# Attention and MLP under a scheduler: w_in's loads placed ahead of block 2, attention paced by another rule, and another planned DMA rate

## The chip, the cores and the metric

The kernel runs on one core of a Trainium2 chip. The metric is the device time of one execution in microseconds, the median of five runs. One execution was also taken by the hardware profiler; all times inside the kernel come from it. Of the core's engines, PE is the matrix engine TensorE (PEld its weight loads), DVE is VectorE, ACT is ScalarE, POOL is GpSimd, and SP is the queue engine that issues most DMAs.

## The reference

Inputs are q, k, v of shape (4, 8, 768, 64) in float32 (batch, heads, positions, head dimension), w_in (512, 2048) and w_out (2048, 512). Attention looks at chunks of 32 keys and keeps, for each query, the six chunks with the highest upper bound. Its result, with heads side by side, goes through an MLP with softplus.

```python
k_chunks = k.reshape(B, H, nc, chunk, D)                # chunk = 32, nc = 24
k_min, k_max = np.min(k_chunks, axis=3), np.max(k_chunks, axis=3)
ub = np.sum(np.maximum(q[:, :, :, None, :] * k_min[:, :, None, :, :],
                       q[:, :, :, None, :] * k_max[:, :, None, :, :]), axis=-1)
ub = np.where(causal, ub, -1000000000.0)
top_chunks = np.argsort(ub, axis=-1)[..., -top_k:]      # top_k = 6
scores = scale * np.matmul(q, k.transpose(0, 1, 3, 2))
scores = np.where(sel & (pos[:, None] >= pos[None, :]), scores, -1000000000.0)
attn = softmax(scores)                                  # written out in the reference
x = np.matmul(attn, v).transpose(0, 2, 1, 3).reshape(B * S, H * D)
h = x @ w_in
g = np.maximum(h, 0.0) + np.log1p(np.exp(-np.abs(h)))
return g @ w_out                                        # (3072, 512) float32
```

## The kernel before

The 3072 rows are cut into 12 blocks of 256 queries, three for each batch. For a block, attention works on four pairs of heads (`attend(n, p)`), after a preparation (`prep(n)`) that makes the bounds and the mask, and the MLP makes 16 tiles of 128 hidden features (`mlp_h`) and two tiles of 128 output rows (`mlp_y`). The attention of blocks 0, 1 and 2 is the ramp; the loop then emits the MLP of block n followed by loads, preparation and attention of block n + 3.

**What sets the order.** Nothing is issued where it is written. Every step is a `Task` in a `Graph` with an engine, a planned duration, the tasks it depends on, the buffers it takes and a priority, which is its due time. `Graph.schedule` plays the graph through at build time: whenever an engine is free, it gets the ready task of the lowest priority whose buffers are free. The order that comes out on each engine is the order in the program, and each engine then runs its queue strictly in that order, waiting on semaphores. Planned times never reach the chip; only the order does. A transfer has a planned `dma` time (1.17 for a load of 256 KB, 1.15 for a DMA transpose) and the queues share the DMA engines by packet weights. VectorE operations marked `port=True` and GpSimd's operations are never planned at the same time.

**Due times.** `when_att[n, p]` and `when_mlp[n, i]` come from a loop that deals out units of attention (of blocks 3 to 11) and of the MLP, starting at `MSTART`; it takes a unit of attention as long as the share of attention dealt out is at most `AHEAD` times the share of the MLP:

```python
        if ia < len(a_units) and (im >= len(m_units) or ta / asum <= ahead * tm / msum):
```

`prep(n)` is due 14 ahead of the first attention unit of its block (for the ramp, `RLEAD[n]` ahead), its loads `LEAD` = 18 ahead. `POST[n]` puts back what follows the attention of ramp block n.

**Loads of the ramp.** `ORDER` lists them: `k0` is k of block 0 and so on, `i01` the first half of w_in, `o0` a quarter of w_out. Loads of q, k and v go out from SP (some of block 0's from ACT), the weights from POOL, which converts them to bf16 on the way. A weight that follows a load of q, k or v in the list is put behind a "hold": a copy of one element on POOL (line 428) out of the tile named in `HOLD`, so that POOL issues the weight only when that tile has landed. The other way round, SP's next loads wait for a two-element DMA out of a weight (`hold_sp`, line 434). `LGATE` is such a gate, behind the third quarter of w_out: all loads of blocks 3 to 11 (line 465) depend on it.

**The chain of a block from block 3 on.** Loads (L465) in float32; casts to bf16 on POOL (L472 for q and k, L470 for v); DMA transposes of k (L520) and q (L568) on SP; on DVE the chunks' minima and maxima (L524), their spread into `bd` (L541), the positive and negative parts of q (L577) and copies (L580, L530); the bounds on PE (L597, L598, `ub`); on DVE the causal addition (L604), the eight highest (L613), the comparison with the sixth (L621, L624) that gives the mask in `mr`; a DMA transpose of the mask (L660) and two copies into the q operands (L663). Then `attend`: scores on PE (L700), exponentials on ACT (L709), the causal cut of the last tile by an affine select on POOL (L715), attention times v (L726), normalisation on DVE (L735, L747), and a DMA transpose into x (L763). In the ramp the transposes are PE matmuls (L501, L558, L645, L755).

**The MLP.** `mlp_h`: L783 on PE with w_in, exponential and logarithm on ACT (L789, L793). `mlp_y`: L809 on PE with w_out, a copy on DVE (L814), the store from SP (L819).

**Fillers.** Until the planned time `WARM` = 30, where PE has nothing ready, the scheduler puts a matmul on zeros (L363) into one PSUM bank that is kept spare for it. They stand in the program like any other instruction.

PSUM has eight banks; `PSUM_CAP` limits how many each use may hold (`s` scores, `h` and `y` of the MLP, `o` attention results and bounds, `t` transposes of the ramp).

Of the kernel before, what the change touches and what calls it, by code (L numbers as in the profile page):

```python
# [16 lines left out]
B, H, S, D = 4, 8, 768, 64  # L17
# [3 lines left out]
NP = H // 2  # L21
# [11 lines left out]
NRAMP = 3  # L33
OHP = -97.5
W2 = 18
# [3 lines left out]
TLAT = 1.4  # L39
RLEAD = (0, 0, -1)  # L40
POST = (9, 2, -2)
OPRIO = 15.0
LEAD = 18
BG = 40
DMA_START = 1.3
MSTART = 10.0
AHEAD = 1.16
ORDER = "k0 q0 k1 v0 q1 v1 k2 q2 v2 i01 i23 o0 o1 o2 o3".split()
HOLD = ("k", 2, 1)

# [4 lines left out]
WIDE = {"xf", "kq", "kt", "mt", "oall"}  # L55
PSUM_CAP = {"s": 4, "h": 3, "y": 2, "o": 2, "t": 3, "l": 4, "kq": 4, "kt": 2, "mt": 2, "oall": 2}

# [15 lines left out]
class Graph:  # L73
# [39 lines left out]
    def schedule(self):  # L113
# [8 lines left out]
        def post(at, what, x):  # L122
            nonlocal seq
            seq += 1
            heapq.heappush(events, (at, seq, what, x))
# [35 lines left out]
        def flow(to):  # L161
            nonlocal moved
            while moved < to:
                live = [q for q in queues.values() if q]
                if not live:
                    moved = to
                    return
                slow = {id(q): q[0][2] if len(live) == 1 else q[0][2] + 1 for q in live}
                total = sum(slow.values())
                rate = {id(q): q[0][2] / total for q in live}  # L170
                step = min(min(q[0][0] / rate[id(q)] for q in live), to - moved)
                moved += step
                for q in live:
                    q[0][0] -= step * rate[id(q)]
                    if q[0][0] <= 1e-9:
                        t = q.pop(0)[1]
                        post(moved + t.lat, "landed", t)

# [90 lines left out]
def build(nc, tiles):  # L269
# [16 lines left out]
    for n in range(NRAMP):  # L286
        for p in range(NP):
            when_att[n, p] = t0 + p * (att[n] + 2.5) / NP
        t0 += att[n] + 2.5
    a_units = [(n, p, att[blocks[n][1]] / NP) for n in range(NRAMP, NB) for p in range(NP)]  # L290
    m_units = [(n, i, 13.9 / 16) for n in range(NB) for i in range(16)]
    asum, msum = sum(u[2] for u in a_units), sum(u[2] for u in m_units)
    ahead = AHEAD
    ia = im = 0
    ta = tm = 0.0
    now = MSTART
    while ia < len(a_units) or im < len(m_units):
        if ia < len(a_units) and (im >= len(m_units) or ta / asum <= ahead * tm / msum):
            n, p, d = a_units[ia]
            when_att[n, p] = now  # L300
            ia, ta, now = ia + 1, ta + d, now + d
        else:
            n, i, d = m_units[im]
            when_mlp[n, i] = now
            im, tm, now = im + 1, tm + d, now + d
# [73 lines left out]
    def v_dst(n, t):  # L379
        b, blk = blocks[n]  # L380
        return T("v", b % 2)[:, blk * NT + t, :, 0:D]
# [26 lines left out]
    def landing(nm, n, hh):  # L408
        return [(XF[nm, n, t], u) for t in ([hh] if n == 0 else range(NT)) for u in range(2)]


    def weight(nm, c4, k4, pr, after):
# [13 lines left out]
    def hold_pool(key, pr):  # L426
        b_ = XF[key]
        return [add("POOL", 0.15, lambda: PO.tensor_copy(T("scratch")[0:1, 0:1], T(b_)[0:1, 0:1]), pr,
                    r=[(b_, 0), (b_, 1)], w=["scratch"], name="hold")]

# [5 lines left out]

    gate, key, wgate, prev = (), None, (), []
    for k_, what in enumerate(ORDER):
        pr = -100 + k_ * 5
        if what[0] in "kqv":  # L440
            if len(prev) > 1:
                gate = hold_sp(*prev[-2], pr - 0.5)
            ramp_loads(what[0], int(what[1]), pr, gate)
            key, wgate, prev = HOLD, (), []
        else:
            nm, c4 = {"i": "w_in", "o": "w_out"}[what[0]], int(what[1])
            k4 = len(what) - 1
            if key:
                wgate, key = hold_pool(key, pr), None
            weight(nm, c4, k4, pr if nm == "w_in" else OPRIO + 0.1 * c4, wgate)  # L450
            prev.append((nm, c4))
    LGATE = hold_sp(*prev[-2], pr)

    def loads(n):
        base = when_att[n, 0] - LEAD
        b, blk = blocks[n]
        for i, nm in enumerate("kqv"):
            b_ = None
            if nm != "v":
                b_ = KQ[nm, n] = Buf("kq")  # L460
            for t in range(NT):
                xf = Buf("xf", "l")

                def ld(nm=nm, t=t, xf=xf):
                    SP.dma_start(out=T(xf).rearrange("s (h d) -> s h d", h=H), in_=rows(nm, n, t))  # L465
                add("SP", 0.6, ld, base + i, at=base + 0.5 * i, w=[xf], dma=1.17, lat=0.6, name=f"ld{nm}{n}", after=LGATE)

                def cast(nm=nm, t=t, xf=xf, b_=b_):
                    if nm == "v":
                        PO.tensor_copy(v_dst(n, t), T(xf).rearrange("s (h d) -> s h d", h=H))  # L470
                    else:
                        PO.tensor_copy(T(b_)[:, :, t], T(xf).rearrange("s (p c) -> s p c", p=NP))  # L472
                w = [("v", b % 2, blk * NT + t)] if nm == "v" else [(b_, t)]
                add("POOL", 0.6, cast, base + i + 2, r=[xf], w=w, name=f"c{nm}{n}")

    QAB, X, done = {}, {}, {}


    def prep(n):
        b, blk = blocks[n]  # L480
        i = b % 2
        ramp = n < NRAMP
        pr = when_att[n, 0] - (RLEAD[n] if ramp else 14)
        ncc = (blk + 1) * NCB
# [30 lines left out]
        else:  # L515
# [3 lines left out]
            def tr(ks=ks, kt=kt):  # L519
                SP.dma_start_transpose(T(kt), T(ks).rearrange("s p t c -> s (p t c)"))  # L520
            add("SP", TD, tr, pr, at=pr - 4, r=[(ks, 0), (ks, 1)], w=[kt], dma=1.15, lat=TLAT, name=f"kTd{n}")
            for m in range(2):
# [41 lines left out]
        else:  # L564
            qs = KQ["q", n]

            def tr(qs=qs):
                SP.dma_start_transpose(T(qb).rearrange("d p (t s) -> d (p t) s", t=NT),  # L568
                                       T(qs).rearrange("s p t c -> s (p t c)"))
            add("SP", TD, tr, pr + 0.5, at=pr - 3, r=[(qs, 0), (qs, 1)],  # L570
                w=[(qb, hh, z) for hh in range(2) for z in range(3)], dma=1.15, lat=TLAT, name=f"qTd{n}")
        for hs in ([[0], [1]] if ramp else [[0, 1]]):
# [83 lines left out]
        else:  # L656
            mt = Buf("mt")

            def tr(mt=mt):
                SP.dma_start_transpose(T(mt).rearrange("d p (t s) -> d (p t) s", t=NT),  # L660
                                       T(mr).rearrange("s p t c -> s (p t c)"))
            add("SP", TD, tr, pr + 3, r=[(mr, z) for z in range(3)], w=[mt], dma=1.15, lat=TLAT, name=f"mTd{n}")
            add("DVE", 0.36, lambda: DV.tensor_copy(T(qa)[64:96], T(mt)[64:96]), pr + 3,  # L663
# [15 lines left out]
    def attend(n, p):  # L679
# [82 lines left out]
        elif p == NP - 1:  # L762
            add("SP", TD, lambda: SP.dma_start_transpose(  # L763
                T(x).rearrange("d p (t s) -> d (p t) s", t=NT), T(osb).rearrange("s p t h d -> s (p t h d)")), pr + 1.5,
                r=[(osb, p_) for p_ in range(NP)], w=[(x, p_) for p_ in range(NP)], dma=1.15, lat=TLAT, name=f"oTd{n}")

# [62 lines left out]
    for n in range(NB):  # L829
        m = n + NRAMP  # L830
        mlp_h(n)
        mlp_y(n, lambda u, f2, n=n: when_mlp[n, 8 + u * 4 + f2 // 2] + 4.0)
        if m < NB:
            loads(m)
            prep(m)
            for p in range(NP):
                attend(m, p)
# [107 lines left out]
```

## Time and profile before

| | us |
|---|---|
| median of five runs | 261.76 |
| lowest and highest | 261.42 and 262.15 |
| the profiled execution, its own time | 261.76 |
| its span, first to last instruction | 260.0 |
| PE busy in the span | 253.6 |
| ACT, DVE, POOL busy | 202.0, 148.7, 82.9 |
| PE busy in 0 to 20 of the span | 18.78 |
| PE busy in 80 to 100 and in 120 to 140 | 19.19 and 19.18 |
| PE busy in 240 to 260 | 16.45 |
| granted TensorE clock | 0.998 |
| DMA, mean rate over the span | 153 GB/s |

Matmuls overlap in the pipeline, so PE's busy time says only that one was in flight; what a stretch holds is seen from the starts of its matmuls. DMA is dense in the first 175 us, where loads, weights and transposes lie, and light after.

### The profile page before, as it was taken

What the parts mean: (1) busy time and instruction counts of PE and PEld (TensorE: products, weight loads), DVE (VectorE), ACT (ScalarE), POOL (GpSimd) and SP (SyncE); (2) the same over time, 40 slices, a digit from 0 to 9 for tenths busy, and PEclk for the clock granted to TensorE, in tenths of its full rate; (3) what the DMA queues carried; (4) which work ended last, traced back from release to release, by engine and by line L of the source; (5) the groups of instructions that cost most, each with busy time, mean ns of one, the idle gap of its engine ahead of it and who ended that gap; (6) DMA issues with size and microseconds to landing.
All of it is one profiled execution on the core that took longest, in us unless ns stands there. A gap on an engine that the chain in (4) does not pass through costs nothing.

```text
span 260.0 us, 6806 instructions
## 1 busy us (share of the span) xinstructions
PE 253.6 (98%) x2598; PEld 192.5 (74%) x2598; DVE 148.7 (57%) x554; ACT 202.0 (78%) x365; POOL 82.9 (32%) x177
## 2 busy tenths in 40 slices
PE   8999999999998999998999999999999999999994
PEld 6898997786685776786677779668677778676763
DVE  7699776339686699549986769469344111111101
ACT  5697999978495985999569799849769789766470
POOL 5256520353161550548207262442201111100000
PEclk9999999999999999999999999999999999999999
DMA  7999999799977997999989998683211320120202
GB/s 167 256 239 216 210 199 222 179 137 285 187 205 113 219 239 159 262 219 188 129 201 244 189 259 193 151 206 84 58 67 40 44 81 3 40 83 0 83 0 82
DMA packets 119989, 39.90 MB, mean 153 GB/s; under 512 B 113524, under 2 KB 115828, under 8 KB 119956
## 3 DMA queue, kind: packets, MB, share of 16 engines
q1 hardware_dynamic: 114452, 34.09, 62.8%
q0 software_dynamic: 3392, 4.85, 10.1%
q10 hardware_dynamic: 2112, 0.52, 0.9%
q8 instruction: 20, 0.33, 0.5%
q14 instruction: 13, 0.11, 0.1%
HBM read 27.26 MB, written 6.29 MB: 129 GB/s over the span
## 4 chain that ended last, share of the span: by engine, by line
PE 63%; DVE 4%; DMA 1%; issue 1%; ACT 1%; DVEq 0%
PE ps L809 24%; PE ps L783 23%; PE ps L700 10%; PE ps L726 5%; DMA w<-mr 1%; DVE qpn L577 1%; DVE w L747 1%; PE ps L598 1%; DVE mr L624 1%; ACT pt L709 1%; DVE bd L541 1%; PE ps L597 0%; DVE st L735 0%; DVE yo L814 0%; DVE mr L621 0%
## 5 line engine op out<-in xcount | busy, mean ns | idle before, releaser
L783 PE MATMUL ps<-x,w_in_sb 128*128 128x256 bf16 x768 | 98.9, 272 | 0.0
L809 PE MATMUL ps<-w_out_sb,g 128*128 128x512 bf16 (+1 forms) x400 | 97.9, 370 | 0.0
L709 ACT ACTIVATE pt<-ps 128x512 bf16<-128x512 f32 (+1 forms) x192 | 90.1, 619 | 5.3 <-PE ps L700 4.9
L789 ACT ACTIVATE e<-ps 128x512 f32<-128x512 f32 x96 | 57.8, 644 | 36.3 <-PE ps L783 34.3
L783 PEld LDWEIGHTS <-w_in_sb 128*128 128x128 bf16 x768 | 72.5, 98 | 15.9
L715 POOL TENSOR_SCALAR_AFFINE_SELECT pt<-pt 128x256 bf16<-128x256 bf16 x96 | 39.4, 417 | 110.6 <-ACT pt L709 110.4
L809 PEld LDWEIGHTS <-g 128*128 128x128 bf16 x400 | 37.4, 98 | 24.2
L793 ACT ACTIVATE g<-e 128x1024 bf16<-128x1024 f32 x48 | 52.5, 1094 | 1.1
L814 DVE COPY yo<-ps 128x512 f32<-128x512 f32 (+1 forms) x25 | 16.7, 668 | 45.8 <-PE ps L809 45.7
L735 DVE RECIPROCAL st<-ps 128x4 f32<-128x4 f32 x48 | 8.5, 178 | 42.2 <-PE ps L726 32.3
L700 PE MATMUL ps<-qab,kb 128*128 128x256 bf16 x192 | 30.6, 259 | 0.0
L726 PEld LDWEIGHTS <-pt 128*128 128x128 bf16 x672 | 26.4, 97 | 4.2 <-issue 0.2
L700 PE MATMUL ps<-qab,ka 96*128 96x256 bf16 x192 | 28.2, 259 | 0.7 <-DVE qab L663 0.7
L726 PE MATMUL ps<-v,pt 128*128 128x65 bf16 x672 | 28.1, 193 | 0.0
L472 POOL CAST w<-w 128x512 bf16<-128x512 f32 x36 | 22.6, 642 | 9.1 <-DMA w<-in_k_dram 7.2
L524 DVE TENSOR_REDUCE kx<-w 128x32 bf16<-128x1024 bf16 x18 | 21.2, 1209 | 1.5 <-DMA w<-w 1.4
L700 PEld LDWEIGHTS <-ka 96*128 96x128 bf16 x192 | 17.1, 97 | 6.5 <-issue 1.0
L363 PE MATMUL ps<-zero 128*128 128x256 bf16 x122 | 19.6, 297 | 1.1 <-DVE zero L333 1.1
L700 PEld LDWEIGHTS <-kb 128*128 128x128 bf16 x192 | 16.5, 97 | 5.2
L470 POOL CAST v<-w 128x512 bf16<-128x512 f32 x18 | 11.1, 615 | 15.9 <-DMA w<-in_v_dram 15.9
L747 DVE TENSOR_TENSOR w<-ps,st 128x256 bf16<-128x256 f32 x36 | 15.2, 422 | 1.3
L363 PEld LDWEIGHTS <-zero 128*128 128x128 bf16 x122 | 12.2, 107 | 3.2 <-DVE zero L333 1.1
(64 smaller groups left out, 178.2 us busy)
## 6 DMA issues: line engine op xcount, KB each, us to landing
w<-in_v_dram SPq DMA_DIRECT2D x24, 256.0 KB, 4.5
out_dram<-yo SPq DMA_DIRECT2D x23, 256.0 KB, 2.2
w<-in_k_dram SPq DMA_DIRECT2D x22, 256.0 KB, 3.7
w<-in_q_dram SPq DMA_DIRECT2D x22, 256.0 KB, 4.3
w_in_sb<-in_moe_w_in_dram POOLq DMA_DIRECT2D x2, 1024.0 KB, 11.2
w_out_sb<-in_moe_w_out_dram POOLq DMA_DIRECT2D x4, 512.0 KB, 18.6
w<-in_k_dram SPq DMA_DIRECT2D x2, 128.0 KB, 2.8
w<-in_k_dram ACTq DMA_DIRECT2D x2, 128.0 KB, 3.3
```

The lines of the kernel that those rows point to most:

```text
L363: PE.matmul(T(Fill)[:, 0:256], T("zero")[:, 0:128], T("zero"), start=True, stop=True)
L472: PO.tensor_copy(T(b_)[:, :, t], T(xf).rearrange("s (p c) -> s p c", p=NP))
L524: DV.tensor_reduce(T(kx)[:, m].rearrange("d p (t c) -> d p t c", t=NT), T(kt).rearrange("d (p t) (c s) -> d p t c s", t=NT, s=CH), axis=AX ...
L700: PE.matmul(T(sp)[:, z * QB:z * QB + QB - q0], kk[r0:r1, p, (j + z) * 128:(j + z + 1) * 128], qq[r0:r1, p, q0:QB], start=True, stop=True)
L709: AC.activation(T(pt)[:, j:j + 2].rearrange("k j c -> k (j c)")[:, 0:w], T(sp)[:, 0:w], ACT.Exp, scale=SCALE)
L715: PO.affine_select(out=diag, in_=diag, compare_op=ALU.is_ge, fill=0.0, base=0, channel_multiplier=-1, pattern=[[0, 2], [1, 128]])
L726: PE.matmul(o[:, u, h], T(pts[h])[:, j, c0:c0 + 128], T("v", i)[:, j, 2 * p + h, :], start=(j == 0), stop=(j == t0 + u))
L747: DV.tensor_tensor(dst, o[:, :, :, 0:D], T(st).to_broadcast([128, NT, 2, D]), op=ALU.mult)
L783: PE.matmul(o, T("w_in")[:, dt, ft * 128:(ft + 1) * 128], T(x)[:, dt], start=(dt == 0), stop=(dt == KDM - 1))
L789: AC.activation(T(e)[:, f2 * 2:f2 * 2 + 2].rearrange("f a s -> f (a s)"), T(hp), ACT.Exp)
L793: AC.activation(T(gb)[:, f4 * 4:(f4 + 1) * 4], T(e), ACT.Ln, bias=1.0)
L809: PE.matmul(T(y)[:, 0:w], T(gb)[:, f, u * 128:(u + 1) * 128], T("w_out")[:, f, cs], start=(f == 0), stop=(f == KFF - 1))
```

## The change

Only numbers, one list, one formula and the place of a function change; the operations and their shapes stay. `loads` moves up in the file and gets an option for loads that stand in `ORDER`, which the new list does not use.

- The list: w_in now comes ahead of k, q and v of block 2. So POOL's first hold is on the second tile of q of block 1, SP's loads of block 2 wait for the first half of w_in, and w_out is held by the second tile of q of block 2.
- Pacing: attention of blocks 3 to 11 is spread over the MLP's share after `AOFF` = 16 and until `AEND` = 26 of planned time, in place of the factor `AHEAD`; `MSTART`, `RLEAD`, `POST`, `OHP` get other values, `SHIFT` puts block 2's attention 8 later, and the preparation is due `PLEAD` = 12 ahead.
- Planned DMA times: 1.25 for a load of 256 KB from block 3 on (210 GB/s) and for the DMA transposes.
- PSUM: three banks instead of four for scores, four instead of three for the ramp's transposes.

```diff
-OHP = -97.5
+OHP = -90
...
-RLEAD = (0, 0, -1)
-POST = (9, 2, -2)
-OPRIO = 15.0
+RLEAD = (1, 1, -1)
+POST = (0, 5, -2)
+OPRIO = 15
...
-MSTART = 10.0
-AHEAD = 1.16
-ORDER = "k0 q0 k1 v0 q1 v1 k2 q2 v2 i01 i23 o0 o1 o2 o3".split()
-HOLD = ("k", 2, 1)
+MSTART = 16
+AOFF = 16
+PADD = 0.0
+PLEAD = 12
+AEND = 26
+ORDER = "k0 q0 k1 v0 q1 v1 i01 i23 k2 q2 v2 o0 o1 o2 o3".split()
+HOLDS = [("q", 1, 1), ("q", 2, 1), ("q", 2, 1)]
+SHIFT = (0, 0, 8)
...
-PSUM_CAP = {"s": 4, "h": 3, "y": 2, "o": 2, "t": 3, "l": 4, "kq": 4, "kt": 2, "mt": 2, "oall": 2}
+PSUM_CAP = {"s": 3, "h": 3, "y": 2, "o": 2, "t": 4, "l": 4, "kq": 4, "kt": 2, "mt": 2, "oall": 2}
...
-            when_att[n, p] = t0 + p * (att[n] + 2.5) / NP
+            when_att[n, p] = t0 + SHIFT[n] + p * (att[n] + 2.5) / NP
...
-        if ia < len(a_units) and (im >= len(m_units) or ta / asum <= ahead * tm / msum):
+        if ia < len(a_units) and (im >= len(m_units) or ta / asum <= (tm - AOFF) / (msum - AOFF - AEND)):
...
-                    r=[(b_, 0), (b_, 1)], w=["scratch"], name="hold")]
+                    r=[(b_, 0), (b_, 1), b_], w=["scratch"], name="hold")]
...
-            key, wgate, prev = HOLD, (), []
+            new, wgate, prev = True, (), []
...
-            if key:
-                wgate, key = hold_pool(key, pr), None
+            if new:
+                wgate, new = hold_pool(HOLDS[holds], pr), False
+                holds += 1
...
-                add("SP", 0.6, ld, base + i, at=base + 0.5 * i, w=[xf], dma=1.17, lat=0.6, name=f"ld{nm}{n}", after=LGATE)
...
+                add("SP", 0.6, ld, order + i if early else base + i, at=0.0 if early else base + 0.5 * i, w=[xf], dma=1.25, lat=0.6, name=f"ld{nm}{n}", after=gate if early else LGATE)
...
-        pr = when_att[n, 0] - (RLEAD[n] if ramp else 14)
+        pr = when_att[n, 0] - (RLEAD[n] if ramp else PLEAD)
...
-            add("SP", TD, tr, pr, at=pr - 4, r=[(ks, 0), (ks, 1)], w=[kt], dma=1.15, lat=TLAT, name=f"kTd{n}")
+            add("SP", TD, tr, pr, at=pr - 4, r=[(ks, 0), (ks, 1)], w=[kt], dma=1.25, lat=TLAT, name=f"kTd{n}")
```

The other three kinds of DMA transpose (q, mask, x) get 1.25 in the same way.

## The prediction

> **What bounds the kernel now.** I read the engine totals first, then the chain that ended last, then the waits, then TensorE's timeline where it stalls and the other engines beside it.
>
> ```profile
> PE 253.6 (98%) x2598; PEld 192.5 (74%) x2598; DVE 148.7 (57%) x554; ACT 202.0 (78%) x365; POOL 82.9 (32%) x177
> PE   8999999999998999998999999999999999999994
> PE 63%; DVE 4%; DMA 1%; issue 1%; ACT 1%; DVEq 0%
> L363 PE MATMUL ps<-zero 128*128 128x256 bf16 x122 | 19.6, 297 | 1.1 <-DVE zero L333 1.1
> PE ps L700 <- DVE qab L663: 0.7, 1, 0.7
> PE ps L598 <- DVE qpn L577: 0.6, 1, 0.6
> ```
>
> TensorE is busy to the end and dips in slices 13 and 19 only. So the end moves only by what TensorE issues without need, and by the places where it waits. The first kind is L363, 122 filler matmuls on zeros that the scheduler puts where nothing else is ready in the ramp. Their cost is the step from one to the next, not the mean in that row (matmuls overlap). The second kind is in TensorE's timeline:
>
> ```profile
> 10.47 1.47 PE L363 MATMUL ps<-zero 128*128 128x256 bf16 x12
> ...
> 81.70 1.24 PE L809 MATMUL ps<-w_out_sb,g 128*128 128x512 bf16 x5
> 83.63 0.54 PE L700 MATMUL ps<-qab,ka 96*128 96x256 bf16 x4 [0.69 <-DVE qab L663]
> ...
> 121.33 1.04 PE L783 MATMUL ps<-x,w_in_sb 128*128 128x256 bf16 x8
> 122.63 0.19 PE L597 MATMUL ps<-bd,qpn 128*128 128x32 bf16 x1 [0.26 <-DVE qpn L577]
> 123.38 0.19 PE L598 MATMUL ps<-bd,qpn 128*128 128x32 bf16 x1 [0.56 <-DVE qpn L577]
> ```
>
> Twelve fillers end 1.47 after the first starts and one lasts 0.27 (page: a matmul of 256 columns, 272 ns), so the step is (1.47 - 0.27) / 11 = 0.109 us. Five 512-column matmuls give (1.24 - 0.38) / 4 = 0.216. Five of those from 81.70 would be through at 82.78; the scores of block 4 start at 83.63: 0.85 lost. Eight 256-column steps from 121.33 end at 122.20; block 7's bound matmul starts at 122.63 (0.43 lost) and its partner is 0.73 late again: 1.16. A smaller case at 93.7 (block 5's bounds, the same wait) loses 0.28. Sum: 2.29 us.
>
> Why VectorE is late there is seen beside GpSimd:
>
> ```profile
> 76.67 2.53 POOL L472 CAST w<-w 128x512 bf16<-128x512 f32 x4
> 76.78 0.58 DVE L624 CAST mr<-ub 128x4 bf16<-128x4 f32 x1
> 127.20 0.17 DVE L624 CAST mr<-ub 128x4 bf16<-128x4 f32 x1
> 121.68 2.11 POOL L472 CAST w<-w 128x512 bf16<-128x512 f32 x3
> 121.80 1.53 DVE L577 TENSOR_SCALAR qpn<-qab 128x1024 bf16<-128x1024 bf16 x2
> ```
>
> The same tiny L624 takes 0.17 alone and 0.58 beside GpSimd's casts of the next block's loads; two L577 take 1.53 beside casts, where one alone takes 0.42. Beside GpSimd's affine selects (L715) L624 averages 0.33. So the three stalls are the casts of blocks 5, 6 and 8 running beside the preparation of blocks 4, 5 and 7.
>
> **The change, part by part.** The profiled execution took 261.76 us, which is the median of the runs, with a span of 260.0: 1.76 lie outside the span and stay. The built order of the changed program is known, and I cost it with the steps above.
>
> *Fillers.* 118 instead of 122: 4 x 0.109 = -0.44. All other TensorE work has the same count.
>
> *w_in moved ahead of block 2.* GpSimd's hold used to stand behind all eight selects and a cast of v:
>
> ```profile
> 14.92 1.54 POOL L715 TENSOR_SCALAR_AFFINE_SELECT pt<-pt 128x256 bf16<-128x256 bf16 x4 [2.00 <-ACT pt L709]
> 19.67 0.25 POOL L428 CAST scratch<-w 1x1 bf16<-1x1 f32 x1
> 19.86 1.56 POOL L416 DMA_DIRECT2D w_in_sb<-in_moe_w_in_dram  x2
> DMA to landing us min/median/max: 9.0/11.2/13.4
> ```
>
> It now stands behind the first four selects, so the first half is issued at 14.92 + 1.54 + 0.25 = 16.7 instead of 19.9. In before it landed 9.0 after its issue (28.9), the second half at 20.6 + 13.4 = 34.0, that is 5.1 later. So the first half lands between 16.7 + 5.1 = 21.8 (moving alone, no start-up) and 16.7 + 9.0 = 25.7 (as crowded as before); block 2's loads, which shared the queues, are now gated behind it, but the DMA still has to start up: I take 24.9, nearer to the crowded row. Who asks: in the new order the first scores of block 1 stand 228.3 us of TensorE work ahead of the last matmul, the first w_in matmul (h0) 227.4. Block 1's chain (q1, bounds, mask) is untouched, and its first scores ran at 24.2 in before. So h0 asks at 24.2 + 0.9 = 25.1. Stall: 0 to 0.65; I take 0.1. In before h0 stood 223.4 from the end and ran at 29.8; that it can run earlier is what replaces the 12 fillers that stood after block 1's first scores.
> [...]
>
> *Block 2, w_out and block 3's loads moved back.* SP's gate for k2 and q2 waits for w_in's first half, GpSimd's second hold waits for q2, and queued behind that hold are w_out's four loads, block 2's v casts and all later selects and casts; behind SP's last gate (w_out's third quarter) are block 3's loads and every store. Walk: 24.9 + 0.7 (gate) = 25.6; k2 and q2 get little until w_in is through at 30.0; then four tiles of 256 KB at the 238 GB/s of 10 to 20 us, 1.1 each: 34.4; hold and issue: 34.7. w_out's quarters landed from 34.0 to 45.5 in before, 2.9 each: third quarter at 34.7 + 2 (start-up, an estimate: what 24.9 leaves over 16.7 + 5.1, less than 3.1) + 8.7 = 45.4. Gate 0.7: block 3's first load goes at 46.1; in before it went at 43.3. TensorE needs block 3's bounds 189.8 from the end instead of 190.6, 0.8 later. The cover is that the old loads waited: issued at 43.3, landed a median 3.7 later, and cast by GpSimd only at 50.2 and 52.0, behind selects paced by ScalarE: some 3 us of slack. 2.8 - 0.8 < 3, so 0; without that cover the cost is up to 2.
>
> *Pacing and the 210 GB/s.* Attention is due later against the MLP, preparation starts 12 instead of 14 ahead, every SP transfer is planned as 1.25 instead of 1.15 to 1.17. What counts is the TensorE work that stands between a block's bounds and its first scores, since the mask chain (L604 to L663) runs under it: block 4 8.46 (8.75 before), block 5 9.95 (9.12), block 6 12.1 (9.3), block 7 10.75 (9.72), block 10 10.75 (7.88), block 11 7.80 (8.46). And GpSimd's order: between block 3's selects only one of the four casts that met L624 is left ahead of the last five selects; the two casts of block 8's k have seven selects between them. So:
> - Block 4: four L624 beside selects lose 4 x (0.33 - 0.17) = 0.64 instead of 4 x 0.41 = 1.64. 0.85 - 1.0 + 0.29 less cover = 0.14 if selects are met, 1.14 if casts are: I take 0.5 (-0.35).
> - Block 5: 0.28 stays (0 to 0.9).
> - Block 7: the casts may miss L577 altogether (0) or meet it as before (1.16): 0.6 (-0.56).
> - Block 11: its mask was ready 0.4 before the scores (L663 ends 200.62, scores 201.01); 0.66 less cover leaves 0.25 (+0.25; 0 to 0.7).
> - Scores get three PSUM banks instead of four: ScalarE's exponentials must come free sooner. No wait on them over 0.1 in before; +0.2 (0 to 0.6).
>
> Sum: -0.44 + 0.1 - 0.35 - 0.56 + 0.25 + 0.2 = -0.80. Span 259.2, time 260.96, say 261.0. Ends: all stalls gone, -0.44 - 2.29, 259.0; all upper ends (+0.65 + 0.3 + 0.6 + 0 + 0.7 + 0.6 - 0.44), +2.4 or 264.2, and 2 more with block 3's loads late; these are not met together.
>
> **Rivals.** *Nothing gained:* fillers go, but their time returns as waits: the collisions depend on when loads land, not on the plan; with stalls of 2.7 to 3.1 instead of 2.29 the time is 261.7 to 262.2. For it: in before too GpSimd was meant to be off the port and wasn't. Against: covers grew for blocks 5 to 10.
> *Slower:* block 3's loads come too late. Place: SP's last gate. It decides from a first load later than about 46.5: then each us goes through cast, transposes, L524 and bounds to TensorE, as nothing else is left to issue ahead. At 48 the price is 1.5 less the 0.44: 262.8 and up to 264. For it: a chain of five dependent landings (w_in, q2, w_out). Against: 3 us of slack.
> *All collisions gone:* 259.0 to 259.6. Against: VectorE and GpSimd are no less busy.
>
> **How the numbers follow.** Forecast (259.7 to 261.2) 0.50, collisions gone 0.05, nothing gained 0.27, slower 0.18. 0.2% of 261.76 is 0.52, about what a measurement can tell from no change: faster means under 261.24, slower over 262.28. Faster 0.55, same 0.26, slower 0.19. Range 259.6 to 262.8.
>
> **What would show it.** Right: 118 fillers, none after some 22 us; h0 at 25 to 26; no wait on w_in or w_out; block 3's first load at about 46 and its bounds without a wait; the wait on L577 at block 7 halved. Wrong: an idle TensorE before h0 over 0.7, a wait on block 3's transposes, or new waits on L577 and L663 that sum to over 2.7.

## The result: 0.35% faster, and the profile after

The changed kernel took 261.25 us in the median of its runs (259.69 to 263.06), the kernel before 262.26 beside it (260.62 to 265.81); the ratio is 0.9965, with a 95% interval of 0.9954 to 0.9976. The ratios leave out executions over 1.5% above the fastest of their kernel. Executions scatter by 3 and 5 us, so single profiles are read below for where time goes, and the ratios for how much. The profiled execution after took 261.28 us with a span of 259.6.

From the page of the kernel after: the engine totals, TensorE's busy tenths in 40 slices, the chain that ended last, and the fillers' group.

```profile
PE 252.2 (97%) x2594; PEld 191.4 (74%) x2594; DVE 150.7 (58%) x549; ACT 202.8 (78%) x369; POOL 84.4 (33%) x179
PE   8999998999999999999999999999999999999994
PE 74%; DMA 15%; DVE 4%; SPq 2%; issue 1%; POOL 1%; ACT 0%; DVEq 0%
L366 PE MATMUL ps<-zero 128*128 128x256 bf16 x118 | 17.1, 288 | 1.1 <-DVE zero L336 1.1
```

Slices 13 and 19 are full now; the only dip left after the start is slice 7, at 39 to 45.5 us. DMA's share of the chain rose from 1% to 15%: the chain runs back through w_out's load, the load of q of block 2 and w_in's load, the list's row of dependent landings. How often TensorE waits for each is in the view of waits (engine, line, releaser: us in total, times, longest):

```profile
PE ps L823 <- DMA w_out_sb<-in_moe_w_out_dram: 1.2, 2, 0.8
PE ps L612 <- DVE qpn L591: 0.8, 2, 0.6
PE ps L769 <- DVE osb L761: 0.5, 2, 0.3
```

And TensorE's timeline after (start, us, engine, line, operation, idle before and releaser). From the start of one matmul to that of the next, less the usual step, each wait costs a little more than the idle time shown (0.92 for 0.76 and 0.64 for 0.47 at w_out).

```profile
4.50 1.91 PE L366 MATMUL ps<-zero 128*128 128x256 bf16 x16
...
24.47 0.60 PE L797 MATMUL ps<-x,w_in_sb 128*128 128x256 bf16 x4
...
41.37 1.90 PE L823 MATMUL ps<-w_out_sb,g 128*128 128x512 bf16 x8 [0.76 <-DMA w_out_sb<-in_moe_w_out_dram]
...
47.40 1.02 PE L823 MATMUL ps<-w_out_sb,g 128*128 128x512 bf16 x4 [0.47 <-DMA w_out_sb<-in_moe_w_out_dram]
...
83.81 1.46 PE L823 MATMUL ps<-w_out_sb,g 128*128 128x512 bf16 x6
85.11 0.55 PE L714 MATMUL ps<-qab,ka 96*128 96x256 bf16 x4
...
93.42 0.20 PE L611 MATMUL ps<-bd,qpn 128*128 128x48 bf16 x1
94.17 0.20 PE L612 MATMUL ps<-bd,qpn 128*128 128x48 bf16 x1 [0.55 <-DVE qpn L591]
...
122.68 0.60 PE L797 MATMUL ps<-x,w_in_sb 128*128 128x256 bf16 x4
123.12 0.18 PE L611 MATMUL ps<-bd,qpn 128*128 128x32 bf16 x1
```

(L797 is h, L823 y, L611 and L612 the bounds, L591 the split of q, L769 the ramp's transpose of x, in the numbering after.) h0 runs at 24.5 without a wait. The stalls at blocks 4 and 7 are gone (the scores at 85.11 and the bounds at 123.12 follow without a wait); in their place stand two waits for w_out (0.92 and 0.64 us lost), two on L769 at 65 and 69 us (0.37 and 0.46) and a larger one at block 5 (0.72). From 30 us on the stalls sum to more than before (3.29 us for 2.56), and the first 30 us make up for it, by a slow start that was shorter in this execution (below) and by the four fillers, 0.44 us. So these two spans (260.0 and 259.6) do not say what the change gains.

GpSimd's timeline shows why w_out is late:

```profile
15.50 0.18 POOL L457 CAST scratch<-w 1x1 bf16<-1x1 f32 x1
15.62 1.54 POOL L445 DMA_DIRECT2D w_in_sb<-in_moe_w_in_dram  x2
...
33.67 0.41 POOL L729 TENSOR_SCALAR_AFFINE_SELECT pt<-pt 128x256 bf16<-128x256 bf16 x1 [0.96 <-ACT pt L723]
35.76 0.18 POOL L457 CAST scratch<-w 1x1 bf16<-1x1 f32 x1 [1.68 <-DMA w<-in_q_dram]
```

The second hold (L457) waits 1.68 us for q of block 2, with the last select of block 1 (33.67) safely ahead of it in the queue. That place in the queue matters below.

### The profile page after: what moved, and what is told of

The parts are those of the page before. It is cut to its first block, busy times and chain, and to the rows that moved or that the text cites. A ratio compares the mean times of both kernels' runs of the same rounds, so it can differ in the third digit from the quotient of the medians.

```text
span 259.6 us, 6793 instructions
## 1 busy us (share of the span) xinstructions
PE 252.2 (97%) x2594; PEld 191.4 (74%) x2594; DVE 150.7 (58%) x549; ACT 202.8 (78%) x369; POOL 84.4 (33%) x179
## 4 chain that ended last, share of the span: by engine, by line
PE 74%; DMA 15%; DVE 4%; SPq 2%; issue 1%; POOL 1%; ACT 0%; DVEq 0%
PE ps L823 29%; PE ps L797 26%; PE ps L714 11%; PE ps L740 6%; DMA w<-in_q_dram 4%; DMA w_out_sb<-in_moe_w_out_dram 4%; DMA w_in_sb<-in_moe_w_in_dram 3%; DMA w<-w 2%; SPq L401 2%; DVE kx L538 1%; DMA w<-in_k_dram 1%; DVE qpn L591 1%; PE ps L612 1%; PE ps L366 1%; POOL pt L729 1%
## 5 line engine op out<-in xcount | busy, mean ns | idle before, releaser
L797 PE MATMUL ps<-x,w_in_sb 128*128 128x256 bf16 x768 | 101.6, 272 | 0.0
L723 ACT ACTIVATE pt<-ps 128x512 bf16<-128x512 f32 (+1 forms) x192 | 94.2, 610 | 9.2 <-PE ps L714 8.9
L823 PE MATMUL ps<-w_out_sb,g 128*128 128x512 bf16 (+1 forms) x400 | 97.2, 370 | 1.2 <-DMA w_out_sb<-in_moe_w_out_dram 1.2
L797 PEld LDWEIGHTS <-w_in_sb 128*128 128x128 bf16 x768 | 72.4, 98 | 15.1
L803 ACT ACTIVATE e<-ps 128x512 f32<-128x512 f32 x96 | 59.8, 646 | 26.5 <-PE ps L797 26.2
L729 POOL TENSOR_SCALAR_AFFINE_SELECT pt<-pt 128x256 bf16<-128x256 bf16 x96 | 40.1, 424 | 122.4 <-ACT pt L723 122.2
L823 PEld LDWEIGHTS <-g 128*128 128x128 bf16 x400 | 36.7, 98 | 26.6 <-DMA w_out_sb<-in_moe_w_out_dram 1.0
L828 DVE COPY yo<-ps 128x512 f32<-128x512 f32 (+1 forms) x25 | 16.7, 669 | 40.9 <-PE ps L823 40.8
L714 PE MATMUL ps<-qab,ka 96*128 96x256 bf16 x192 | 29.1, 259 | 0.0
L366 PE MATMUL ps<-zero 128*128 128x256 bf16 x118 | 17.1, 288 | 1.1 <-DVE zero L336 1.1
L627 DVE MAX8 ub<-ub 128x8 f32<-128x24 f32 (+2 forms) x160 | 14.5, 161 | 0.3
L366 PEld LDWEIGHTS <-zero 128*128 128x128 bf16 x118 | 11.4, 103 | 2.7 <-DVE zero L336 1.1
```

The lines of the kernel that those rows point to most:

```text
L366: PE.matmul(T(Fill)[:, 0:256], T("zero")[:, 0:128], T("zero"), start=True, stop=True)
L714: PE.matmul(T(sp)[:, z * QB:z * QB + QB - q0], kk[r0:r1, p, (j + z) * 128:(j + z + 1) * 128], qq[r0:r1, p, q0:QB], start=True, stop=True)
L723: AC.activation(T(pt)[:, j:j + 2].rearrange("k j c -> k (j c)")[:, 0:w], T(sp)[:, 0:w], ACT.Exp, scale=SCALE)
L729: PO.affine_select(out=diag, in_=diag, compare_op=ALU.is_ge, fill=0.0, base=0, channel_multiplier=-1, pattern=[[0, 2], [1, 128]])
L797: PE.matmul(o, T("w_in")[:, dt, ft * 128:(ft + 1) * 128], T(x)[:, dt], start=(dt == 0), stop=(dt == KDM - 1))
L803: AC.activation(T(e)[:, f2 * 2:f2 * 2 + 2].rearrange("f a s -> f (a s)"), T(hp), ACT.Exp)
```

## The experiments

**Which part brings the gain.** The change has three: the list with its holds, offsets and PSUM banks, the pacing, and the planned DMA times. Four kernels leave out one or two. The edits, against the change:

```diff
 ramp_alone and no_pace (before's pacing)
-MSTART = 16
+MSTART = 10.0
+AHEAD = 1.16
-PLEAD = 12
+PLEAD = 14
-  ... ta / asum <= (tm - AOFF) / (msum - AOFF - AEND)):
+  ... ta / asum <= AHEAD * tm / msum):
 ramp_alone and no_dma (before's planned times; five places)
-  dma=1.25
+  dma=1.17      # loads; 1.15 for the DMA transposes
 pace_dma (before's list)
-ORDER = "k0 q0 k1 v0 q1 v1 i01 i23 k2 q2 v2 o0 o1 o2 o3".split()
-HOLDS = [("q", 1, 1), ("q", 2, 1), ("q", 2, 1)]
+ORDER = "k0 q0 k1 v0 q1 v1 k2 q2 v2 i01 i23 o0 o1 o2 o3".split()
+HOLDS = [("k", 2, 1)]
 # and before's OHP, RLEAD, POST, PSUM_CAP; SHIFT = (0, 0, 0)
```

> The change's list of loads, holds, offsets and PSUM caps, with before's pacing and before's DMA times: 123 fillers. Theory (the gain is four fillers, -0.44, plus stalls moved about, so a kernel is ahead only as far as its fillers fall): 123 x 0.109 is +0.1 over before; TensorE work between bounds and first scores grows at blocks 4 to 6 (12.5, 11.7 and 11.0 us for 8.75, 9.1 and 9.3), which takes away block 4's 0.85 to 1.65: ratio to before 0.994 to 1.000. Rival A (the list alone carries the gain of the whole change): ratio as the change's own, 0.9954 to 0.9976, with w_in's first half landing near 24 and no wait at h0. Rival B (the list only costs, by the waits on w_out of 0.9 and 0.6, and the pacing pays for it): 1.002 to 1.006.

> The change without its pacing (attention of later blocks again due by 1.16 times the share of the MLP, from 10 us on, preparation 14 ahead), but with its list and its DMA times: 123 fillers; covers at blocks 4 to 8 of 11.8, 12.3, 11.2, 9.3 and 10.4 us. Theory: the list without the pacing saves no filler (+0.1), the stalls at blocks 4 and 5 go and block 7's stays as in before: ratio to before 0.995 to 1.001, between before and the change. Rival A (the list carries the gain): 0.9954 to 0.9976. Rival B (without the pacing the scores of later blocks crowd ScalarE while GpSimd is late, so the list costs): 1.002 to 1.008.

> The change without its longer DMA times (1.17 and 1.15 again, which is about what 238 GB/s gives): 118 fillers, work between bounds and scores at blocks 4 to 7 of 10.7, 10.4, 15.4 and 9.0 us for the change's 8.5, 9.95, 12.1 and 10.75. Theory: the fillers' 0.44 stays gained, block 7's stall (0.4 to 1.2) may return, block 5's 0.7 goes: ratio to before 0.994 to 1.000. Rival A (the 1.25 us is what keeps VectorE ahead of TensorE): 1.000 to 1.004, with new waits of over 0.5 at the bounds or scores of two or more blocks. Rival B (the DMA time does nothing): within 0.1% of the change itself.

> Before's list, holds, offsets and PSUM caps, with the change's pacing and its DMA times: 122 fillers, w_in behind block 2. Theory: no fillers saved, the first 60 us as in before (h0 near 29.8, waits on w_out absent), and blocks 4 to 7 with more work between bounds and scores (11.8, 10.0, 10.6 us; block 7 9.4): only the stalls of 83 and 122 us go, up to 2.0 of 2.3: ratio 0.993 to 0.999. Rival A (the list carries the gain): 0.999 to 1.002, as the stalls come back at other blocks. Rival B (pacing carries it): 0.9954 to 0.9976 or below.

| kernel | list | pacing | DMA times | median us | ratio to before (95%) |
|---|---|---|---|---|---|
| ramp_alone | new | old | old | 267.17 | 1.0181 (1.0161 to 1.0201) |
| no_pace | new | old | new | 264.71 | 1.0071 (1.0053 to 1.0088) |
| no_dma | new | new | old | 262.98 | 0.9986 (0.9960 to 1.0011) |
| pace_dma | old | new | new | 261.60 | 0.9967 (0.9939 to 0.9995) |
| the change | new | new | new | 261.25 | 0.9965 (0.9954 to 0.9976) |

For ramp_alone every expectation failed, and for no_pace only the last rival's number came, by another cause than it named: with before's pacing the list costs 1.8%, and 0.7% with the longer DMA times. For pace_dma the theory's range held, and so did that of the rival that pacing carries the gain; for no_dma the theory's range held. Pacing and DMA times without the list give as much as the whole change. Beside the new list the pacing is worth 1.1% (with the longer DMA times) to 2.0% (without). So the list brings nothing to the end here and the pacing pays; the expected gain of moving w_in ahead is missing. The rival that the list carries the gain is refuted. What the DMA times are worth beside the new pacing stays unclear: the interval of no_dma touches that of the change. Not separated are pacing and DMA times on the old list, and the list from its offsets and PSUM banks.

Beside the new list, the gain of the pacing does not lie in the stalls at blocks 4 and 7. They are gone in no_pace too, with the old pacing: from 75 us on TensorE's largest waits there are 0.31 us at 142 and 0.17 at 81. With the old list, pace_dma's profile has them gone as its theory said, but loses 0.86 at 94 to 96 and 0.49 at 118 instead, and its span (260.1) is before's; where its 0.3% lies it does not show.

Where the list loses without the pacing is seen in no_pace. GpSimd's timeline, then TensorE's (line numbers are one higher there):

```profile
36.57 0.18 POOL L458 CAST scratch<-w 1x1 bf16<-1x1 f32 x1 [0.36 <-DMA w<-in_q_dram]
36.70 3.02 POOL L449 DMA_DIRECT2D w_out_sb<-in_moe_w_out_dram  x4
39.69 0.45 POOL L730 TENSOR_SCALAR_AFFINE_SELECT pt<-pt 128x256 bf16<-128x256 bf16 x1
```

```profile
40.20 0.45 PE L741 MATMUL ps<-v,pt 128*128 128x65 bf16 x9 [1.19 <-POOL pt L730]
42.43 0.61 PE L824 MATMUL ps<-w_out_sb,g 128*128 128x512 bf16 x1 [1.78 <-DMA w_out_sb<-in_moe_w_out_dram]
```

One affine select of block 1 is left behind the second hold and w_out's four issues of 0.76 us each. Attention (L741) waits for it, then y for w_out: 1.36 + 1.95 us lost, against 0.92 + 0.64 in the change, where all of block 1's selects stand ahead of the hold. That is 1.75 of the 2.8 us by which the ratios of the two differ (0.0106 of 262.3); four waits between 67 and 69 us add 1.3. This is read from one profile each; no run moves the select alone. ramp_alone shows the same two waits (0.99 and 1.92 lost) and further ones at 72 to 77 us in front of the bounds and scores of block 3, some 3 us in all between 70 and 80.

no_pace's profiled execution took 267.61, 2.9 us above its median, and shows one thing more. The table of windows (us, then busy time and count of each engine, granted clock, DMA share, GB/s):

```profile
40.00:41.00 1.00, 0.45 (x9) 0.33 (x9) 0.47 (x3) 0.96 (x3) 1.00 (x3) 1.00 1.25 204
41.00:42.00 1.00, 0.00 (x0) 0.00 (x0) 0.33 (x1) 0.99 (x2) 0.25 (x1) 0.62 1.21 199
42.00:43.00 1.00, 0.57 (x1) 0.28 (x3) 0.00 (x0) 0.96 (x3) 0.00 (x0) 0.50 1.16 194
...
47.00:48.00 1.00, 1.00 (x7) 0.69 (x6) 0.00 (x0) 0.02 (x1) 0.00 (x0) 0.50 1.22 201
48.00:49.00 1.00, 1.00 (x8) 0.60 (x7) 0.00 (x0) 0.58 (x1) 0.00 (x0) 0.96 1.24 207
```

The granted clock was half from about 41.2 to 48.1 us (worked out from the 0.62 and 0.96 of the windows from 41 and 48): it fell inside the second wait, when TensorE had lost some 2 us, and stayed down 5.7 us after the wait. In ramp_alone's profile the pair of waits was 2.9 us and the clock stayed at 1.00 throughout 42 to 48.

**What a filler is worth.** Two kernels drop fillers when the order is emitted, with all else frozen: few_fill keeps only the first 59 of 118, early_fill leaves out 8 of the 16 that stand between the two transposes of block 0's k.

```diff
     for t in order:
+        if t.name == "fill":
+            fills += 1
+            if fills > 59:                        # few_fill
+            if 13 < fills <= 29 and fills % 2:    # early_fill
+                continue
         t.fn()
```

> The changed kernel with its order, but only the first 59 of its 118 fillers are emitted; the 59 from the first scores of block 0 on are left out. Theory (a filler costs its 0.109 us where TensorE runs behind its data, so four fewer gave 0.44): what stands behind them starts as soon as its data is there. In the changed kernel's profile the mask of block 1 was ready at 21.87 and its transposes ran at 22.43, so 0.3 to 0.6 us are gained. Rival 1 (fillers only stand in for waits; the ramp is bound by VectorE and ScalarE): no change within 0.2. Rival 2 (the fillers keep TensorE's clock up): gaps of about 1 us between 13 and 23 us bring the slow step of 0.21 for 256 columns back, and the time is 0.5 to 3 us longer.

> The changed kernel with its order, but every second of the 16 fillers between the two first transposes of block 0's k is left out (8 fewer). In before's profile the fillers there ran at a step of 0.213 until 6.4 us and the second transposes began at 7.31, the last q transposes at 9.82; in the changed kernel's profile the step was 0.109 from 4.2 on, they began at 6.25, and the last q transposes waited for q's landing at 9.20. Theory (the first 10 us differ between executions by how long the clock stays slow, not by the change): without these fillers the slow executions lose up to 0.6 less and the fast ones nothing: the time falls by 0.1 to 0.4, and its spread gets smaller. Rival (the slow step follows from how the kernel begins, every time): 0 or 0.6 in all executions. Second rival: with fewer fillers the clock rises later and the time is longer.

few_fill: 261.59 us, 0.9927 (0.9897 to 0.9957). early_fill: 260.18 us (259.64 to 260.41), 0.9862 (0.9826 to 0.9899). The 59 late fillers are 6.4 us of steps and leaving them out moved the time by nothing that shows. The 8 early ones are 0.9 us at the fast step and brought 0.6 to 1.0%: against the change's 0.9965, or against hold_q20 (below) and few_fill, 0.9922 and 0.9927, which were measured beside it. That is more than the theory's 0.1 to 0.4 us. In few_fill the waits they had covered come out, and the clock drops among them (timeline of few_fill):

```profile
22.09 0.29 PE L769 MATMUL ps<-ident,osb 128*128 128x128 bf16 x2 [0.88 <-DVE osb L761]
...
23.76 0.40 PE L769 MATMUL ps<-ident,osb 128*128 128x128 bf16 x2 [0.70 <-DVE osb L761]
23.95 0.95 PE L714 MATMUL ps<-qab,ka 96*128 96x256 bf16 x4
```

Block 1's first scores start at 23.95, where the change had them at 23.64. This execution was 0.72 behind at block 0's first mask transposes (11.86 for 11.14), so 0.41 was caught up without the fillers. The clock takes it back: the four scores take 0.95 for 0.55, at a granted clock of 0.50 in 24 to 27 us, and by 28 us TensorE is 1.8 behind the change. The second rival named this mechanism, though not the time. The end does not show it, because the change waits for w_out where few_fill does not: at 50 us it is 0.4 behind. All eight executions of few_fill have a mean granted clock of 0.986 to 0.993, where the twelve of the change measured once more (below) have 0.997 to 1.000, so the late fillers do hold the clock up. The early fillers are another case: there TensorE's steps are still long. In the lines shown, 16 fillers take 1.91 us after, a step of 0.109; in before's profile they took 2.75, as 8 of the steps were 0.213 still. Over the 14 profiles of this study the step fell to 0.109 at any time between 4.2 and 7.1 us, so the same 16 fillers hold TensorE for 1.75 (after) to 2.9 us (ramp_alone), and where the step is long they run past the landing of q of block 0 (its last transposes start at 9.82 without a wait in before's profile, at 9.24 after a wait of 0.20 in the one after). With 8 fewer, TensorE waited for that landing in this execution (timeline of early_fill; L823 is y, which asks for w_out):

```profile
8.04 0.27 PE L572 MATMUL ps<-identf,w 128*128 128x128 f32 x1
9.76 0.55 PE L572 MATMUL ps<-identf,w 128*128 128x128 f32 x3 [1.45 <-DMA w<-in_q_dram]
...
39.49 1.91 PE L797 MATMUL ps<-x,w_in_sb 128*128 128x256 bf16 x16
41.51 1.90 PE L823 MATMUL ps<-w_out_sb,g 128*128 128x512 bf16 x8
...
46.91 1.03 PE L823 MATMUL ps<-w_out_sb,g 128*128 128x512 bf16 x4
```

But that is not where this profile gains. q landed 0.5 later than in the change's profile (9.76 for 9.24), and at 40 us TensorE is 0.79 behind it (39.49 for 38.70). It gets ahead afterwards: 0.28 us are lost for w_out where the change lost 1.56, and nothing at the two L769 near 65 and 69 us where the change lost 0.83; the third quarter of w_out landed at 46.7 for 47.4. Why w_out lands sooner without the early fillers no run shows. That the 8 fillers cost time is shown; that they cost it at the landing of q is not.

**Whether that needs the list.** The same 8 fillers left out of pace_dma:

> Before's list with the change's pacing and DMA times (ratio 0.9967), and 8 of the 16 fillers between the transposes of block 0's k left out as well. Theory (the 16 fillers, issued while a step may still be 0.213, run past the landing of q0's second tile near 9.7 us, whatever the list): the end comes 0.7 to 2 earlier as it did with the change's list, ratio 0.988 to 0.994, and the times lie closer together. Rival (the early fillers pay only with the change's list, where the waits on w_out shrink): 0.995 to 1.000.

262.01 us, 0.9968 (0.9936 to 0.9999): no gain over pace_dma's 0.9967. The rival holds. With the old list TensorE runs into w_in (timeline of early_pace, and of the kernel before profiled once more, 262.71 us):

```profile
28.09 0.38 PE L714 MATMUL ps<-qab,ka 96*128 96x256 bf16 x2
30.91 0.61 PE L797 MATMUL ps<-x,w_in_sb 128*128 128x256 bf16 x4 [2.44 <-DMA w_in_sb<-in_moe_w_in_dram]
```

```profile
30.09 1.16 PE L783 MATMUL ps<-x,w_in_sb 128*128 128x256 bf16 x9 [0.41 <-DMA w_in_sb<-in_moe_w_in_dram]
```

With the old list w_in lands at 28.9 to 30.9 (in pace_dma h0 starts at 30.02), and in early_pace, where the scores before h0 ran 1.5 us earlier than in the kernel before, TensorE only waited for it longer; with the new list it landed at 23.82. (early_pace's profile is of an execution of 264.39, and its clock was 0.50 in 32 to 35 us, after that wait.) So the list seems to be worth this: it takes away a floor near 30 us that TensorE reaches only if something else brings it there sooner. That rests on one profile of early_pace and on the ratios.

**Whether w_out's hold is the loss at 41 us.** hold_q20 lets the second hold read the first tile of q of block 2 instead of the second, the order unchanged.

```diff
+        c_ = XF["q", 2, 0] if key == ("q", 2, 1) else b_
-        ... T(b_)[0:1, 0:1]), pr,
+        ... T(c_)[0:1, 0:1]), pr,
```

> The order of every engine is that of the changed kernel; only the tile that w_out's hold reads is another: the first tile of block 2's q instead of the second. In the changed kernel's profile that hold ran at 35.76, when the second tile had landed; the select ahead of it ended at 34.08 and the first tile had landed by then. Theory (w_out's late landing costs TensorE 0.92 + 0.64 = 1.56 us at 40.3 and 46.7): the four loads go out 1.7 us earlier, both waits vanish, and the time falls by 1.0 to 1.6 against the changed kernel, 2.0 to 2.5 against before. Rival (those waits only stand in for later ones, as the chain of block 3's loads, casts and bounds ends last anyway): both waits vanish, but waits of blocks 3 and 4 grow by as much, and the time falls by less than 0.4 against the changed kernel. Second rival: block 2's q lands later beside w_out and its transposes (TensorE, about 38) wait 0.5 to 1.5 instead.

261.27 us, 0.9922 (0.9889 to 0.9955), where the change measured once more (below) has 0.9952 (0.9925 to 0.9979): not told apart, and the ratios cannot decide between the theory (1.0 to 1.6 us) and the first rival (under 0.4). The trace can: the waits did not vanish, 0.84 and 0.36 us are lost at the same two places. w_out was issued 1.3 us earlier (34.55 for 35.88), but its third quarter landed no sooner (47.4 in both). At 41 us the wait moved to another releaser (timeline of hold_q20):

```profile
41.70 1.90 PE L824 MATMUL ps<-w_out_sb,g 128*128 128x512 bf16 x8 [0.68 <-ACT g L808]
...
47.45 0.81 PE L824 MATMUL ps<-w_out_sb,g 128*128 128x512 bf16 x3 [0.20 <-DMA w_out_sb<-in_moe_w_out_dram]
```

y of block 0 needs w_out and g, and ScalarE's last g of the block, queued behind casts of block 2's k, ended at 41.26 after, 0.06 before w_out landed at 41.32. The trace names the later of two causes that lie side by side.

> The 8 early fillers left out, and w_out's hold on q2's first tile instead of its second, the order otherwise the change's. Theory (with the early fillers gone w_out's last waits are 0.28 at 41 and none at 47, and ScalarE's g of block 0 ends within 0.1 of w_out's landing): nothing more to win, ratio 0.984 to 0.989. Rival (w_out's load is what still sets the end of block 0's y): 0.978 to 0.983.

Together with the 8 early fillers left out: 259.64 us, 0.9873 (0.9830 to 0.9917), the theory's range.

**Whether a GpSimd cast is the whole stall at block 5.** On top of early_fill, the first cast of block 6's k moves behind the select that follows it:

```diff
+    two = [t for t in order if t.name == "ck6"]
+    order.remove(two[0])
+    order.insert(order.index(two[1]), two[0])
```

> As the run that leaves out 8 early fillers (its ratio was 0.986), and GpSimd's first cast of block 6's k moved behind the select that followed it, so that it no longer runs beside L591 of block 5. Theory (GpSimd's cast stretches VectorE's L591, and that is the whole stall): the two L591 take 0.85 to 1.05 together for 1.30, and TensorE's 0.72 before L612 near 92.5 falls to 0.1 to 0.4; the end comes 0.3 to 0.6 earlier, ratio 0.982 to 0.986. Rival (L591 is late because of what stands ahead of it on VectorE, L538 and L761): the stall stays at 0.6 or more.

259.65 us, 0.9870 (0.9826 to 0.9914): the ratio missed the range named, and is no better than early_fill's 0.9862, but the place is clear. Timelines of early_fill (VectorE, GpSimd, TensorE), then of late_cast6:

```profile
91.91 1.30 DVE L591 TENSOR_SCALAR qpn<-qab 128x1024 bf16<-128x1024 bf16 x2
92.14 0.80 POOL L436 CAST w<-w 128x512 bf16<-128x512 f32 x1
92.52 0.20 PE L611 MATMUL ps<-bd,qpn 128*128 128x48 bf16 x1
93.27 0.20 PE L612 MATMUL ps<-bd,qpn 128*128 128x48 bf16 x1 [0.55 <-DVE qpn L591]
```

```profile
90.79 0.89 DVE L591 TENSOR_SCALAR qpn<-qab 128x1024 bf16<-128x1024 bf16 x2
92.38 2.31 POOL L436 CAST w<-w 128x512 bf16<-128x512 f32 x4
91.40 0.20 PE L611 MATMUL ps<-bd,qpn 128*128 128x48 bf16 x1
91.73 0.20 PE L612 MATMUL ps<-bd,qpn 128*128 128x48 bf16 x1
```

The two L591 took 0.89 instead of 1.30, and 0.41 of the 0.72 lost before L612 went: the theory's place and size. The four casts, run together after it, took 2.31 us, where the profile after has 0.80 and 1.72. The remaining 0.31 is L591's own time: it starts 0.6 ahead of L611 and takes 0.89.

**Both kernels once more**, for what is their own and what chance:

> The kernel before, unchanged, for a second profile. Theory (the length of the slow start is chance): the step of the fillers falls to 0.109 at another time than 6.4, between 3 and 8 us, and block 1's first scores (24.18) move by up to 0.7 with it; the three waits of 0.85, 0.28 and 1.16 on VectorE come back within 0.5 in sum. Rival (the first profile was like all): all within 0.1.

262.71 us. The stalls at blocks 4 and 7 are back, not of the same size: 1.48 us idle before block 4's scores (0.69 in the first profile), 0.27 and 0.56 at block 7 (0.26 and 0.56); 0.41 for w_in is new (none), and the 0.28 lost at block 5 is absent. The slow step ended at much the same time as in the first profile (the second transposes of block 0's k at 7.15 for 7.31).

> The changed program as it is, once more. If waits on w_out of 0.9 and 0.6, two on L769 of some 0.4 and one at block 5 of 0.7 are its own, they are there again within 0.3 each and the ratio to before is 0.994 to 0.999. If they were accidents of the first profile, their sum (3.1) falls below 2 or they stand at other blocks. The step of the fillers should fall from 0.213 to 0.109 at some time between 4 and 7 us, not always the same.

261.31 us, 0.9952 (0.9925 to 0.9979). The lost times: for w_out 0.58 and 0.61, at block 5 0.72, on L769 0.48 once and on L612 of block 3 0.51. But for the last, these are the first profile's waits, each within 0.4; the other one on L769, 0.37 at 65 us, did not come back. Within the 0.3 expected are three of the five.

Both early_hold and late_cast6 beat the change, measured beside them, by 0.8%, and the kernel before by 1.3%; neither is told apart from early_fill, so the early fillers left out are what they show.

## Why the prediction was right, and where not

The time forecast was 261.0 and 261.25 came; the direction and the range held. The bound that the prediction set for faster, 261.24, was measured from a kernel before of 261.76; beside the 262.26 measured here, the interval of the ratio lies wholly below 1. Step by step:

- **Fillers.** The count held (118, the last at 23.4 us instead of some 22). That four fewer are worth 4 x 0.109 was believed too easily: few_fill took 59 out for nothing, early_fill 8 for 0.6 to 1.0%. Neither came as a count times a step.
- **w_in ahead.** GpSimd issued at 15.62 (said 16.7), the first half landed at 23.82 (24.9), h0 ran at 24.47 (25.1) without a wait. The two issues took 0.77 us each while VectorE was busy for 1.50 of 1.60 us, and the landing came 8.2 after the issue, sooner than before's 9.0.
- **Block 2 and w_out.** This is the term that was mis-sized. The walk had q of block 2 through at 34.4, w_out issued at 34.7 and its third quarter down at 45.4, and by it no wait on w_out. Measured: 35.70, 35.88 and 47.36, and 1.56 us lost. The walk missed 1.3 us ahead of q's landing, when two GpSimd transfers into ka and kb (issued at 28.6 and 30.0) shared the DMA, which is argued, not tested, and 0.8 in w_out's own load. y asked for the third quarter at 46.8: a walk of three landings with a margin of 1.4 us should have had a price.
- **Block 3's loads.** First load at 48.02 (46.1), past the 46.5 from which the slower rival was to decide, and its price of 1.5 us did not come: 0 at block 3's bounds in the profile after, 0.51 in the second. The slack was larger than the 3 us given.
- **Blocks 4 and 7.** Better than priced: 0 where 0.5 and 0.6 stood (before's 0.85 and 1.16 are gone). The collisions went as said: two of block 4's L638 (before's L624) took 0.39 and 0.37 beside selects and two 0.16, where before had four of 0.58 beside casts, and block 7's two L591 took 0.97 for 1.53, beside selects and no cast. But beside the new list the pacing was not needed for it: no_pace has no stall there either.
- **Block 5.** 0.28 was to stay; it became 0.72. The mechanism, GpSimd's casts beside L591, is the prediction's own, and late_cast6 shows it (two L591 in 0.89 without a cast beside them, 1.30 with one). The step only looked at the cover between bounds and scores, and this cast meets the split of q ahead of the bounds.
- **Block 11 and the PSUM banks.** 0.09 each (0.25 and 0.2).
- **Not in the sum.** Two waits on L769, 0.83 us; and the start, where the step of 0.213 lasted to 6.4 us in before's profile and 4.2 after; by the second transpose of block 0's k that is 1.06 us (7.31 and 6.25).

That 261.0 came so near has luck in it. The terms that were too small sum to 2.83 us (w_out 1.56, block 5 0.44, L769 0.83), those too large to 1.47 (blocks 4 and 7, block 11, the PSUM banks, h0), and the first 40 us, which had no term but for h0 and the fillers, lost some 0.9 less than in before's profile: 0.4 in all, which is what the span missed by (259.6 for 259.2). And the forecast started from a profile of before that was 0.5 us faster than the median of its 87 runs, while the profile after is at its own median: measured by medians the gain is 1.0 us and not 0.5. The deeper error is in the parts: the sum put nearly half of the gain down to w_in ahead of block 2 (the fillers it replaces), and the list without the pacing loses 1.8%.

## What to carry to other kernels

Where a queue holds an instruction that waits for a landing, list what is queued behind it and who needs that; here one select of 0.4 us left behind a hold went with 1.36 us lost on TensorE. Price a part of a change by what it frees, too: here an earlier load was worth nothing by itself, and a shorter start nothing without the earlier load. Test filler work where it stands: the late ones were worth nothing and the early ones 0.6 to 1.0%, and a profile of the start alone would not have shown it.

## What the runs showed of the hardware

- TensorE's first steps are 0.213 us for a matmul of 256 columns and fall to 0.109 at a time that differs between executions, also of the same kernel (the second transposes of block 0's k start at 6.25 and 6.48 in the two profiles of the change). In 14 profiles it lay between 4.2 and 7.1 us into the span, 3.1 to 6.0 after the first matmul, which stands at 1.12. The granted clock reads 1.00 in every window from 1.1 to 7 us in before, after, ramp_alone, no_pace and early_fill; only the steps show the difference. What sets the time no run shows.
- The granted clock was halved after short waits in three profiles and stayed at 1.00 in a fourth, and the length of the waits does not tell them apart. In no_pace it was half for 7 us when 1.4 us and then 0.8 us of a second wait had been lost, with 0.45 us of work between; in ramp_alone two waits in the same place, 0.99 and 1.92 us lost, left it at 1.00 in 42 to 48; in early_pace it was 0.50 in 32 to 35 us after a single wait of 2.6 us; and in few_fill no wait was over 1.1 us, but TensorE was busy for only 0.22 of the us from 21 and 0.30 of that from 23, and the clock was 0.50 from 24 to 27.
- A GpSimd cast of 128x512 and VectorE's L591 beside each other both took longer: 0.80 us for the cast (the median of 24 in the profile after is 0.61), 1.30 for two L591 (after, early_fill) instead of 0.89 with no cast beside them (late_cast6).
